# Two small reads move from SyncE's DMA queue to GpSimd's, behind its fill of a zero tile

## The chip, the cores and the metric

The kernel runs on one core of a Trainium2 chip. The metric is the device time in microseconds (us) of one execution; lower is better. Three runs of the kernel before gave 217.78 us as the median, from 217.74 to 218.26.

A core has five engines, which work through their own instruction lists in order and wait for each other through semaphores: TensorE (PE, with PEld for its weight loads), VectorE (DVE), ScalarE (ACT), GpSimd (POOL) and SyncE (SP). SP computes nothing here; it issues transfers. ACT and POOL issue a few transfers too. All transfers run on the core's 16 DMA engines. SBUF is the on-chip memory with 128 partitions, PSUM the memory that TensorE writes to.

## The reference

An attention with polynomial features feeds a token-mixing block. For batch 4, heads 4, sequence 1088 and head size 32:

```python
a = einsum('rd,bhsd->bhsr', S1, x); b = einsum('rd,bhsd->bhsr', S2, x)   # r = 8
phi(x) = outer product of a and b over r, flattened to 64 features
kv  = einsum('bhsf,bhsd->bhfd', phi(k), v);  z = sum over s of phi(k)
att = (phi(q) @ kv) / (phi(q) . z + 1e-6)                    # (4, 4, 1088, 32)
x   = att laid out as (4, 1088, 128)
theta = x @ w_theta
y = w_tok_r @ (x * cos(theta)) + w_tok_i @ (x * sin(theta))  # over the sequence
u = x + y
out = u + max(u @ w_ch, 0)
```

q, k and v are float32. S1, S2 (8 x 32 each) and the weights (two 1088 x 1088, two 128 x 128) come as float64. [...]

## The kernel before, in words

**Order of the work.** The function describes the work as 1,020 operations (`op(engine, duration, function, writes, reads, due, ...)`), numbered in the order of the calls. Two tables written into the file, `ORDER` and `STARTS`, give the order in which the operations are issued and a planned start in hundredths of a us. Each engine runs its operations in that order and waits where data is missing. `STARTS` also decides which buffer of a class an operation gets, and how many filler matmuls TensorE does between operations. The dependencies between them are found from the buffers that they read and write.

**Loads.** q, k and v of a batch come as one transfer of 576 KB each (line 671; the keys of batches 0 and 1 by ACT's queue, line 668; the queries of batch 3 in another layout, line 663). A second copy of the keys of batches 1 to 3 comes at line 714. The token weights come as 17 rows of 1088 KB (line 642, tile zs), the square weights as one transfer of 256 KB (also line 642). SP issues all of them but the two at line 668, in the fixed order. A transfer on SP's or ACT's queue takes one of eight semaphores in turn, so the ninth must wait until the first has landed, the tenth for the second, and so on; POOL's transfers have eight of their own. Those of POOL at line 393 add to what lies in their target.

**The small matrices.** Lines 435 to 472 bring in S1 and S2. `read_heads(E, i0, i1)` issues two reads on the engine E: at line 444 both matrices, transposed by the host to 32 rows of 16 numbers, go to four groups of 32 partitions of tile st (128 rows of 128 bytes, 16 KB); at line 446 S2 as it is goes to 8 partitions (2 KB). DVE clears st first (line 452). Then ACT makes float32 numbers of it (line 459), DVE shifts, masks and joins the words (lines 463 to 468, shown as L383 and L386, the lines of the helpers), ACT converts the low parts (line 471), DVE multiplies (L379). The result is tile sp. From it come the scaled matrices (lines 498 to 540) and sbk, the block matrix with which TensorE makes the features of the keys (`kfeatures`).

```python
src = s_t.rearrange("d t r -> d (t r)").unsqueeze(0).to_broadcast((i1 - i0, D, 2 * R))
E.dma_start(dst[i0 * D:i1 * D, 0:2 * R], src)
if i1 == H:
    E.dma_start(dst[0:R, 2 * R:NS], s_2)
```

**The stages.** Until about 78 us the kernel loads, makes the features, the sums over the keys, the levels of the queries and the attention, and turns the rows of token weights into float32 as they arrive: ACT makes two parts of each row (lines 643 and 645), DVE joins them. TensorE begins the mixing of batch 0 as rows become ready. Then the mixing (`mix_row`, `winograd` for the pair of batches 2 and 3, seven products in place of eight) keeps TensorE occupied up to about 210 us. `mix_out`, `done` and `finish` add x, do the last product and store.

**At the start.** POOL makes an identity matrix (masks.py, tile ident) and fills the tile idle with zeros (line 430, operation 0 of the list). TensorE multiplies these zeros as a warm-up from then on (line 428). ACT issues the keys of batches 0 and 1 and loads an activation table. ACT's first real operation is the sum of squares of batch 0's keys (line 693); the next one in its list is line 459.

Of the kernel before, what the change touches and what calls it, by code (L numbers as in the profile page):

```python
# [138 lines left out]
)  # L139
WARM = 0  # L140
FILL = 5.0
LOAD_LEAD = 60.0
RAW_LEAD = 30.0
CHAINS = ((0,), (1,), (2, 3))
QPOOL = (False,) * 4
# [167 lines left out]
def kernel(  # L313
# [12 lines left out]
    B, _, NC, H, D = q.shape  # L326
# [1217 lines left out]
```

## Time and profile before

| what | value |
|---|---|
| median of 3 runs | 217.78 us (217.74 to 218.26) |
| the profiled execution, its own time | 217.81 us |
| its span, from the first to the last instruction | 215.9 us |
| mean granted TensorE clock | 0.995 |
| PE busy | 208.9 us, 97% of the span |
| DVE busy | 174.3 us, 81% |
| ACT busy | 114.5 us, 53% |
| POOL busy | 59.7 us, 28% |
| SP's DMA queue (q1) | 22868 packets, 31.86 MB |
| ACT's DMA queue (q10) | 3600 packets, 1.62 MB |
| POOL's DMA queue (q0, software) | 1552 packets, 3.25 MB |
| read from HBM | 29.84 MB |

How to read what follows. Line numbers (L459) are those of the kernel. "q" behind an engine's name means its sequencer, which issues transfers and waits. A row of a timeline has the start in us from the first instruction, the duration, the engine, the line, the operation, the tile written and the tiles read, and, in square brackets, how long the engine had been idle before and what ended that. The duration of a transfer's issue is that of the issuing instruction; when the data has landed is told by the semaphore, which the trace holds too. The packets that the DMA engines moved are recorded with queue, start, duration and size. The chain of waits is followed back from the last instruction, at each step to what released it. Averages over the span mix the stage that loads and prepares (to 78 us) with the one in which TensorE multiplies (78 to 210 us).

### The profile page before, as it was taken

The page shows a single profiled execution, that of the slowest core. Times are in us where ns is not written, and L with a number is a line of the kernel's source. Part 1 is how long each engine was busy: PE and PEld are TensorE (multiplying, and loading weights), DVE is VectorE, ACT ScalarE, POOL GpSimd, SP SyncE. Part 2 cuts the span into 40 slices and gives each one's busy share as a digit, 9 for nine tenths or more (in the row PEclk, how much of TensorE's full clock was granted, in tenths as well). Part 3 has the DMA queues.
Part 4 walks back from the last instruction along what each step waited for, and adds up shares of the span by engine and source line. Part 5 has one row for each costly group of instructions (what it writes and reads, how often), then busy time and mean ns, then how long its engine had stood idle before and what let it go on. Part 6 is the DMA issues. An engine that isn't in the chain of part 4 may idle for free.

```text
span 215.9 us, 5832 instructions
## 1 busy us (share of the span) xinstructions
PE 208.9 (97%) x2396; PEld 152.8 (71%) x2396; DVE 174.3 (81%) x343; ACT 114.5 (53%) x256; POOL 59.7 (28%) x105
## 2 busy tenths in 40 slices
PE   7899999999999999999999999999999999999992
PEld 7677798868866666866668666667677776666781
DVE  1799998999999998999999798885994747456263
ACT  4899989999998895798704233363810000000000
POOL 1272740306400000604004100000006489950403
PEclk9999999999999999999999999999999999999998
DMA  6999999995998993192002402424050420010735
GB/s 222 395 418 419 384 365 420 425 315 97 360 285 267 416 432 145 75 308 45 0 0 32 74 3 112 114 109 112 2 88 15 67 39 0 0 23 8 125 55 103
DMA packets 28046, 37.09 MB, mean 172 GB/s; under 512 B 20564, under 2 KB 23044, under 8 KB 25844
## 3 DMA queue, kind: packets, MB, share of 16 engines
q1 hardware_dynamic: 22868, 31.86, 42.4%
q0 software_dynamic: 1552, 3.25, 7.2%
q10 hardware_dynamic: 3600, 1.62, 2.8%
q8 instruction: 19, 0.31, 0.6%
q14 instruction: 7, 0.06, 0.1%
HBM read 29.84 MB, written 4.00 MB: 157 GB/s over the span
## 4 chain that ended last, share of the span: by engine, by line
PE 63%; DMA 18%; ACT 14%; issue 2%; SPq 1%; DVE 1%; POOL 1%; POOLq 0%; ACTq 0%
PE ps L399 61%; DMA zs<-w_tok 13%; DMA big<-k_l 5%; ACT big L645 4%; ACT big L643 3%; ACT lv L1056 1%; PE ps L1131 1%; ACT big L1021 1%; ACT g L1199 1%; ACT g L1202 1%; ACT g L1205 1%; ACT g L1203 1%; POOL out L1299 1%; SPq L671 0%; ACT g L1135 0%
## 5 line engine op out<-in xcount | busy, mean ns | idle before, releaser
L399 PE MATMUL ps<-big,zs 128*128 128x384 f32 (+2 forms) x380 | 110.5, 436 | 0.0
L399 PEld LDWEIGHTS ps<-big,zs 128*128 128x128 f32 x380 | 66.9, 190 | 32.5
L379 POOL TENSOR_TENSOR big<-big,big 128x544 f32<-128x544 f32 x16 | 22.1, 1458 | 48.6 <-DVE big L379 44.6
L399 PE MATMUL ps<-big,big 128*32 128x32 f32 (+2 forms) x352 | 22.8, 234 | 0.0
L643 ACT ACTIVATE big<-zs 128x1088 f32<-128x1088 f32 x17 | 20.9, 1231 | 1.5 <-DMA zs<-w_tok 0.9
L379 DVE CUSTOM_DVE_ANT_0 big<-big,big 128x2176 uint16<-128x2176 uint16 x17 | 21.5, 1275 | 0.0
L645 ACT ACTIVATE big<-zs 128x1088 int32<-128x1088 uint32 (+1 forms) x18 | 21.4, 1194 | 0.3 <-DMA zs<-w_tok 0.3
L1338 ACT COPY big<-ps 80x256 f32<-80x256 f32 x1 | 0.4, 368 | 39.6 <-DMA out<-g 39.6
L399 PEld LDWEIGHTS ps<-big,big 128*32 128x32 f32 (+1 forms) x352 | 15.3, 124 | 6.8 <-issue 0.8
L1276 ACT COPY g<-ps 128x384 f32<-128x384 f32 (+1 forms) x6 | 2.5, 466 | 23.4 <-PE ps L399 23.4
L379 DVE TENSOR_TENSOR big<-big 128x544 f32<-128x544 f32 x8 | 9.5, 1204 | 5.6 <-PE ps L399 5.6
L383 DVE TENSOR_SCALAR big<-big 128x1088 int32<-128x1088 int32 x17 | 12.2, 719 | 0.0
L379 POOL TENSOR_TENSOR mf<-mv,sm 128x32 f32<-128x32 f16 (+1 forms) x3 | 0.8, 262 | 39.1 <-DVE sm L379 39.1
L428 PE MATMUL ps<-idle 128*128 128x112 bf16 (+1 forms) x67 | 10.0, 312 | 1.3 <-POOL idle L430 1.3
L379 DVE TENSOR_TENSOR g<-lv 128x768 f32<-128x768 f32 x12 | 11.1, 950 | 0.1
L399 PEld LDWEIGHTS ps<-w,big 128*128 128x128 f32 (+1 forms) x76 | 9.8, 189 | 1.4
L379 DVE TENSOR_TENSOR big<-big,hf 128x1152 f32<-128x1152 f32 x8 | 10.7, 1351 | 0.0
L399 PE MATMUL ps<-w,big 128*128 128x128 f32 (+1 forms) x76 | 10.5, 278 | 0.0
L399 PE MATMUL ps<-sbk,g 128*128 128x64 f32 x72 | 10.0, 276 | 0.3 <-ACT g L793 0.3
L379 DVE TENSOR_TENSOR zs<-zs,g 128x384 f32<-128x384 f32 (+2 forms) x24 | 9.8, 447 | 0.2
L386 DVE SCALAR_TENSOR_TENSOR big<-ps,even,big 128x384 f32<-128x384 f32 (+1 forms) x10 | 4.8, 493 | 6.3 <-PE ps L399 6.2
L1199 ACT ACTIVATE g<-ps 128x384 f32<-128x384 f32 x12 | 5.9, 504 | 7.3 <-PE ps L399 7.3
(199 smaller groups left out, 379.2 us busy)
## 6 DMA issues: line engine op xcount, KB each, us to landing
zs<-w_tok SPq DMA_DIRECT2D x17, 1088.0 KB, 10.6
big<-k_l SPq DMA_DIRECT2D x5, 576.0 KB, 13.2
big<-v_l SPq DMA_DIRECT2D x4, 576.0 KB, 15.6
big<-q_l SPq DMA_DIRECT2D x3, 576.0 KB, 10.7
big<-hf POOLq DMA_DIRECT2D x3, 576.0 KB, 10.0
far<-zs SPq DMA_DIRECT2D x3, 576.0 KB, 2.8
zs<-far SPq DMA_DIRECT2D x12, 144.0 KB, 4.3
big<-k_l ACTq DMA_DIRECT2D x2, 576.0 KB, 4.4
```

The source lines that it names most:

```text
L379: eng.tensor_tensor(out=o, in0=a, in1=b, op=f)
L383: (eng or V).tensor_scalar(out=o, in0=a, scalar1=s1, scalar2=s2, op0=op0, **kw)
L386: (eng or V).scalar_tensor_tensor(out=o, in0=a, scalar=s, in1=b, op0=op0, op1=op1)
L399: T.matmul(o, lhs, rhs, start=start, stop=stop, skip_group_check=True)
L428: T.matmul(nowhere()[:, :n], idle()[:, 0:P], idle()[:, :n], start=True, stop=True, skip_group_check=True)
L643: op("A", 0.22 + n * 0.0009, lambda: A.activation(dfn(), words_of(raw(), n)[1].bitcast(F32), AF.Prelu, scale=2.0**-112, alpha=-(2.0**32)), ...
L645: op("A", 0.22 + n * 0.0009, lambda: A.activation(stp(), words_of(raw(), n)[0].bitcast(U32), AF.Copy, scale=2.0**-29), [stp], [raw])
L1021: op("A", act(GW) + 0.1, lambda g=g, tr=tr: A.activation(f()[:, g * GW:(g + 1) * GW], tr(), AF.Copy, scale=s()[:, 0:1]), [(f, g)], [tr, (s ...
L1056: op("A", act(480), lambda g=g, lp=lp: A.copy(lv().rearrange("p l (c n) -> p l c n", n=HR)[:, :, g * GC:(g + 1) * GC], lp().rearrange("p c ...
L1131: T.transpose(tr()[:, i * P:(i + 1) * P], qp()[:, i * H + 2 * n:i * H + 2 * n + 2].rearrange("p h i j -> p (h i j)"), ident())
L1199: op("A", act(GW), lambda cs=cs, th=th: A.activation(cs()[:, 0], th(), AF.Copy, bias=ROUND), [(cs, 0)], [th])
L1276: op("A", act(w), lambda: A.copy(u(), yp()[:, :w]), [uT], [yp])
```

## The change

The two reads at lines 444 and 446 are issued by POOL instead of SP. Operation 0, POOL's fill of the zero tile, is moved ahead in the list, so that it still comes first on POOL; its planned start changes to 0.90 us, the other operations keep theirs. SP's list is the same but for the two reads: its first transfer is now the keys of batch 3.

```diff
 ORDER = (
-    29, 32, 4, 2, 5, 0, 1, 3, 34, 30, 356, 50, 33, ...
+    29, 32, 4, 0, 2, 5, 1, 3, 34, 30, 356, 50, 33, ...
 STARTS = (
-    73, 73, 90, 92, 103, 130, 170, 220, 358, ...
+    73, 73, 90, 90, 92, 103, 170, 220, 358, ...
...
-        op("S", 0.1, lambda: read_heads(SY, 0, H), [(st, 0)], [], due=-4000.0, lk=H + 1)
+        op("S", 0.1, lambda: read_heads(G, 0, H), [(st, 0)], [], due=-4000.0, lk=H + 1)
```

Of the operations named: 29 and 32 are ACT's key loads, 4 clears st, 0 fills the zero tile, 2 sets constants on DVE, 5 is the pair of reads, 1 is the warm-up, 3 the first activation, 34 SP's load of batch 3's keys, 30 that of batch 0's queries.

118 rows, old and new, of tables (ORDER, STARTS) are left out of this document.

## The prediction

> **What bounds the kernel now.** I read the chain of waits first, then the busy time by stage, then the two timelines of ScalarE (ACT) and VectorE (DVE) over the first 40 us, and last the DMA packets of the first 8 us. In the chain of waits (start, us, what) these pieces are the frame:
>
> ```profile
> 3.63 11.58 DMA big<-k_l
> 15.22 16.38 DMA zs<-w_tok
> 31.63 0.62 ACT big L643
> ...
> 123.58 86.46 PE ps L399 x601
> ```
>
> The end is set by TensorE, which runs almost without a hole from 78 us on. What precedes it is set elsewhere. The busy times by stage (stretch, its length, then busy PE, PEld, DVE, ACT, POOL) say where:
>
> ```profile
> 6.60:15.00 8.40, 7.44 (x166) 5.73 (x165) 7.73 (x26) 7.92 (x24) 4.23 (x16) 1.00 1.03 417
> 15.00:31.60 16.60, 16.31 (x303) 13.22 (x301) 16.18 (x37) 15.26 (x40) 7.86 (x22) 1.00 1.03 393
> 35.00:78.00 43.00, 42.63 (x773) 32.22 (x775) 42.24 (x79) 40.74 (x82) 8.00 (x17) 1.00 0.94 324
> ```
>
> DVE is busy 42.24 of the 43.00 us before the TensorE stage (the PE column holds idle-time matmuls too), and DMA runs at a share of 1.03 up to 31.6 us. So before 78 us a delay of DVE or ACT has nothing to hide under, except where they wait for something else. The timelines of both show every such place of 0.5 us or more between 4 and 40 us (start, duration, group, then idle before it and its releaser):
>
> ```profile
> 4.56 1.17 ACT L693 ACTIVATE big<-big 128x1152 f32<-128x1152 f32 x1 [1.44 <-DMA big<-k_l]
> 6.37 0.24 ACT L459 ACTIVATE sp<-st 128x48 f32<-128x48 f32 x1 [0.55 <-DMA st<-s]
> ...
> 31.63 1.23 ACT L643 ACTIVATE big<-zs 128x1088 f32<-128x1088 f32 x1 [0.58 <-DMA zs<-w_tok]
> ```
>
> ```profile
> 6.65 0.19 DVE L383 TENSOR_SCALAR sp<-sp 128x48 int32<-128x48 int32 x1 [4.49 <-ACT sp L459]
> ...
> 35.10 0.46 DVE L383 TENSOR_SCALAR big<-lv 128x576 f32<-128x576 f32 x1 [0.56 <-ACT lv L1056]
> ```
>
> So the small read, which lands in tile st, gates both: ACT L459 starts 0.09 us after its landing at 6.28, and DVE 0.28 us after that start. From 6.65 to 34.55 DVE has no hole. At 31.05 ACT runs out of work and waits 0.58 for a weight row, and DVE then waits 0.56 for ACT. **The rule I use:** if the first stage starts D later, the first 0.55 us of D vanish in those two waits, whose end is set by DMA; the rest reaches the end one for one.
>
> **The change, part by part.** *SP loses two issues.* The issues before (SP's own queue; start, duration):
>
> ```profile
> 0.98 0.74 SPq L444 DMA_DIRECT2D st<-s_t  x1
> 1.78 0.44 SPq L446 DMA_DIRECT2D st<-s  x1
> 2.27 0.38 SPq L671 DMA_DIRECT2D big<-k_l  x1
> ```
>
> SP waited for DVE's clearing of st (ends 0.95); its entry semaphore came at 0.64, as ACT's did, and ACT issued at 0.72. So SP's first big load (keys of batch 3, 576 KB) moves from 2.27 to about 0.72, 1.55 us. That buys no transfer time by itself: the packets show ACT's two key loads filling all 16 engines from 1.76 to about 5.3 us, and no SP packet before 5.23, though the small reads had been issued by 2.22. Later issues wait for landings eight DMAs back (w_sq at 4.55, a q load at 6.12); with two DMAs fewer these waits lift earlier, but always behind a backlog. Hence 0 for the rest of SP's queue. One gain is possible: over 5.25 to 6.25 us the packets carry some 0.11 MB less than at the 390 GB/s after it, 0.28 us, in the stretch with the 136 small packets. It counts only if the first stage isn't late.
>
> *The price on ACT's first load.* Batch 0's keys (issued by ACT at 0.72, landed 4.54) now meet SP's 576 KB issued in the same 0.01 us. ACT's second load, which today stands in line behind the first, lands from 5.59 to 6.21: that is what batch 0's keys get if SP's load goes first or the two share the engines. Bounds: 0 to +1.67 us. I take 5.9, the middle of 5.59 to 6.21, because two of the three orders give it: L693 then starts 5.92, ACT is free 1.26 later (as 4.56 to 5.82 today), at 7.18, so D = 7.18 - 6.37 = 0.8. The second key load would land at about 8.2 instead of 6.2 and is used at 8.42: covered by ACT's own work, which is late too.
>
> *POOL gets two issues.* It is free at once after its start-up:
>
> ```profile
> 0.86 0.42 POOL L430 MEMSET idle<- 128x384 bf16 x1
> 1.34 0.28 POOL masks.py:199 TENSOR_SCALAR_AFFINE_SELECT ident<-ident 128x128 f32<-128x128 f32 x1
> 8.00 0.79 POOL L379 TENSOR_TENSOR s<-sp 128x16 f32<-128x16 f32 x1 [6.37 <-DVE sp L379]
> ```
>
> Issues start at 1.3 to 1.6 us; one of 128-byte rows (L1299) takes 0.60 to 0.70, so the second starts at 1.9 to 2.3. TensorE's warm-up waits for the fill alone, which stays ahead; the identity (first used 4.86) has 2 us to spare even behind the issues; POOL's next work waits for the read anyway. What the trace lacks is a small POOL read under a full DMA. The nearest rows (KB each, us to landing) bound it:
>
> ```profile
> big<-hf POOLq DMA_DIRECT2D x3, 576.0 KB, 10.0
> ...
> out<-g POOLq DMA_DIRECT2D x7, 48.0 KB, 2.5
> ```
>
> From idle engines 2.0 is the shortest L1299 landing: 1.9 + 2.0 = 3.9 at best. Beside full engines a 576 KB accumulating transfer took 10.0: 2.3 + 10.0 = 12.3 at worst. In packets, those three loaded transfers sent their first one 4.1 to 4.6 us after the issue, against 1.4 to 1.8 idle, and then took turns with SP's. The 128-byte rows of POOL's stores go out as packets of 3072 bytes (24 rows at once), SP's one by one at 128 bytes, so I count the read as one packet per engine, not 32 turns. First packet 1.9 + 4.1 to 2.3 + 4.6 = 6.0 to 6.9, plus 0.5 to the semaphore (5.76 to 6.28 today): 6.5 to 7.4. I take 7.0: D = 7.0 + 0.09 - 6.37 = 0.7.
>
> A rule speaks for the order before: the Trainium skill, DMA: Bandwidth & Descriptors, Issuing engine by pattern, gives simple loads to Sync and calls its path generally faster, with about 1 us to the first byte from GpSimd against 0.6. By that the read would be 0.4 later, plus 0.3 for the later issue: 7.0, an estimate from that page and the start times; the trace's own rows (1.4 to 1.8 idle against 1.05 for ACT's first load) agree in sign.
>
> *Sum.* The two delays overlap: ACT needs both, so the later counts. I take D = 0.95, a little over the larger (0.8) since either may be the later one. Past the slack: 0.95 - 0.55 = **+0.4 us**. The profiled execution took 217.81 (span 215.9 and 1.9 around it), 0.03 over the median 217.78: **218.2 us**.
>
> **The rivals.** *Nothing is lost* (217.8): ACT's load goes first and the read lands by 6.8, so D is under 0.55 and the wait for the weight row swallows it. For it: the queues of ACT and SP so far served whole loads in order. Against it: SP's load is no longer issued later.
>
> *The read is late by a whole turn* (slower, 219.2): it must queue behind what the engines hold and then give way again between its own packets and semaphores. Price: first packet at 2.3 + 4.6 = 6.9, then some of the 1.1 to 2.1 us between the first and the last semaphore of those loaded transfers, say 1.3, so 8.2: D = 1.9, +1.4. If its 32 rows each waited for a 4608-byte packet (0.178 us), 32 x 0.19 = 6 us more than the 6.0 of a first packet: 12, near the worst row, +5.2, 223. It decides from a landing at about 7.5 on. For it: 10.0 against 2.5 above. Against it: the 3072-byte packets.
>
> *The stream starts fuller* (faster, 216.9): between 1.75 and 3.0 us the engines moved 229 KB where 475 KB would fit, 0.63 us. Two loads at once might fill that; with the 0.28 above, the weight row would land 0.9 sooner, at 30.7, and ACT and DVE, 0.55 earlier through an early read, would use it. It decides when L643 starts before 31.0. Against it: the first packets took 0.4 to 0.9 us each instead of 0.178, a slow start that more requests need not cure. The Trainium skill, same page, Queues, rings and completion order, has each engine go round-robin between queues by packets. By that the small read passes the backlog and lands near 4.5, which helps this rival, though batch 0's keys then share with SP's load. Today's SP packets, 3 us behind ACT's, don't show such turns; POOL's do.
>
> **How the numbers follow.** Forecast 0.44, nothing lost 0.16, read late 0.32, fuller start 0.08. What this kernel's measurement tells from no change is about 0.3%, 0.65 us. The forecast case spans +0.1 to +0.9 (D of 0.65 to 1.45) and passes 0.65 in a fifth of its chance: slower 0.32 + 0.09 = 0.41; within 0.44 x 0.8 + 0.16 = 0.51; faster 0.08. The range 217.3 to 219.6 leaves out some 0.06 below and 0.13 above (the 12 us landing and its neighbours).
>
> **What would show it.** L693's start (4.56 now; 5.9 forecast; unchanged if ACT's load goes first); L459's start (6.37; 7.1 to 7.5) and whether st or L693 released it; DVE's first L383 moved alike; the waits at 31.63 and 35.10 gone with those starts moved by 0.4; packets of the software queue at 6 to 7 us, few and large. I'm wrong if L459 moves and the waits at 31.63 and 35.10 stay, since then DMA was not what ended them, or if L459 is on time and the time still moves.

## The result and the profile after

The changed kernel takes 220.6 us (median of 6 executions, 219.91 to 223.01), the kernel before 217.98 beside it on the same chip (6, 217.74 to 218.26). The ratio is 1.0126, 95% interval 1.0097 to 1.0156: slower by 2.75 us, where 0.4 was forecast. The profiled execution is the shortest of the six: 219.91, span 218.0. The ratios are those of undisturbed executions alone, which in some experiments puts the median of all above the ratio.

SP's first load and POOL's first issue stand where the forecast had them, POOL's second 0.17 us behind its bounds of 1.9 to 2.3 (timelines of SP and POOL after; start, duration):

```profile
0.72 0.40 SPq L671 DMA_DIRECT2D big<-k_l  x1
```

```profile
1.58 0.88 POOL L444 DMA_DIRECT2D st<-s_t  x1
2.47 0.55 POOL L446 DMA_DIRECT2D st<-s  x1
```

What came of them is in the timelines of ACT and DVE after, at the instructions shown of before:

```profile
6.47 1.16 ACT L693 ACTIVATE big<-big 128x1152 f32<-128x1152 f32 x1 [3.31 <-DMA big<-k_l]
...
8.78 0.25 ACT L459 ACTIVATE sp<-st 128x48 f32<-128x48 f32 x1 [1.05 <-DMA st<-s]
...
33.48 1.24 ACT L643 ACTIVATE big<-zs 128x1088 f32<-128x1088 f32 x1
```

```profile
9.06 0.19 DVE L383 TENSOR_SCALAR sp<-sp 128x48 int32<-128x48 int32 x1 [6.90 <-ACT sp L459]
...
37.15 0.46 DVE L383 TENSOR_SCALAR big<-lv 128x576 f32<-128x576 f32 x1
```

Batch 0's keys release L693 at 6.47 instead of 4.56. When ACT is through with them, it waits another 1.05 us for the small read, and L459 starts at 8.78 instead of 6.37: **D is 2.41 us**. L643 and DVE's second mark have no bracket any more: both waits are gone, as the rule demands. L643 is 1.85 later than before (2.41 less its wait of 0.58 would be 1.83), DVE's mark 2.05 (1.86 by the rule), and the profiled execution ends 2.10 later. The chain of waits after says the same in fewer words:

```profile
2.47 6.23 DMA st<-s
...
29.45 7.07 PE ps L399 x119
...
125.57 86.46 PE ps L399 x601
```

The two long pieces of key and weight loads that stood in the chain of before are not in it; a DMA of 2 KB is, with 6.23 us. The last piece, TensorE's 86.46 us of mixing, is as long as before and starts 1.99 later. By stage, the loss is all at the front (after; stretch, length, then busy PE, PEld, DVE, ACT, POOL):

```profile
6.60:15.00 8.40, 8.15 (x150) 6.43 (x152) 5.52 (x20) 6.87 (x18) 2.10 (x5) 1.00 1.03 411
15.00:31.60 16.60, 16.17 (x296) 12.61 (x282) 16.06 (x36) 16.02 (x41) 8.36 (x26) 1.00 1.02 400
35.00:78.00 43.00, 43.00 (x743) 32.88 (x740) 42.33 (x79) 41.24 (x86) 7.73 (x17) 1.00 0.93 320
```

DVE does 5.52 us of work in the first stretch where it did 7.73; in the two others it is as busy as before.

The landings, by the semaphores of the trace: batch 0's keys 6.45 (4.54 before), SP's keys of batch 3, issued in the same 0.01 us, 6.25; the first small read 7.97 (6.11), the second 8.69 (6.28). The packets of POOL's queue begin at 6.03. The stream behind is earlier, not later: the keys SP issues fourth land at 13.53 instead of 15.21, and the weight row that L643 waited for at 29.08 instead of 31.61. Nobody can use it, since ACT and DVE are late.

### The profile page after: what moved, and what is told of

It reads as the page before. It is cut to its first block, busy times and chain, and to the rows that moved or that the text cites. A ratio compares the mean times of both kernels' runs of the same rounds, so it can differ in the third digit from the quotient of the medians.

```text
span 218.0 us, 5834 instructions
## 1 busy us (share of the span) xinstructions
PE 210.5 (97%) x2396; PEld 153.8 (71%) x2396; DVE 174.6 (80%) x343; ACT 114.2 (52%) x256; POOL 60.9 (28%) x107
## 4 chain that ended last, share of the span: by engine, by line
PE 86%; ACT 6%; DMA 3%; POOL 1%; DVE 1%; issue 1%; POOLq 0%; ACTq 0%
PE ps L399 81%; DMA st<-s 3%; PE ps L1131 2%; ACT big L693 2%; PE ps L1018 1%; ACT g L793 1%; ACT big L1021 1%; PE ps L428 1%; ACT big L991 1%; ACT big L645 1%; ACT big L643 1%; POOL out L1299 0%; PE ps L1189 0%; POOL st L444 0%; PE ps L790 0%
## 5 line engine op out<-in xcount | busy, mean ns | idle before, releaser
L643 ACT ACTIVATE big<-zs 128x1088 f32<-128x1088 f32 x17 | 20.9, 1231 | 0.5 <-DVE lv L379 0.5
L428 PE MATMUL ps<-idle 128*128 128x112 bf16 (+1 forms) x67 | 10.7, 324 | 1.3 <-POOL idle L430 1.3
```

Source lines behind the costliest of these rows:

```text
L428: T.matmul(nowhere()[:, :n], idle()[:, 0:P], idle()[:, :n], start=True, stop=True, skip_group_check=True)
L643: op("A", 0.22 + n * 0.0009, lambda: A.activation(dfn(), words_of(raw(), n)[1].bitcast(F32), AF.Prelu, scale=2.0**-112, alpha=-(2.0**32)), ...
```

## The experiments

The theory after the result: the loss is D less 0.55, and D comes from two things, keys that share the engines with SP's load, and a read on POOL's queue that lands late under load. Rivals: one of the two alone; the freed SP queue (a stream that collides elsewhere); TensorE's clock.

**1. SP's load ahead of SP's own reads** (the kernel before, operation 5 behind 34). It brings the collision of the key loads without POOL's queue.

```diff
-    29, 32, 4, 2, 5, 0, 1, 3, 34, 30, ...
+    29, 32, 4, 2, 0, 1, 3, 34, 5, 30, ...
```

> The kernel before with one edit: SP issues its first key load ahead of the two small reads, not behind them. The reads stay on SP. This sets the price of the collision of ACT's and SP's first loads by itself. Theory (two delays, the later counts): batch 0's keys share the engines packet by packet with SP's load and land near 6.4 instead of 4.5; the reads stand behind SP's load and land near 7; ACT is free at 7.7, so L459 starts at 7.7 instead of 6.4, and 0.8 to 1.0 us of that reaches the end: 218.8 to 219.0. Rival A (only POOL's read costs, the late keys are covered): no change, 218.0. Rival B (SP's early load is the whole loss): as the changed kernel, 220 or more.

Measured: 219.33 us, ratio 1.0048 (1.0030 to 1.0067). The keys land at 6.32, but the reads at 7.96 and 8.15, later than expected, on SP's queue too. L459 of this kernel:

```profile
8.24 0.25 ACT L459 ACTIVATE sp<-st 128x48 f32<-128x48 f32 x1 [0.64 <-DMA st<-s]
```

So the price of the keys was not measured by itself here. What follows is that POOL's queue isn't needed for a late read: here two reads on SP's queue, issued behind a big load on the same queue, landed 1.85 and 1.87 later than before.

**2. POOL's reads, with SP as late as before.** SP issues the same two reads to a tile that nobody uses, so its big loads start where they did.

```diff
-        st = fixed((NS,), I64, "st")
+        st, st2 = fixed((NS,), I64, "st"), fixed((NS,), I64, "st2")
...
-... lambda: read_heads(G, 0, H), [(st, 0)] ...
+... lambda: (read_heads(G, 0, H), read_heads(SY, 0, H, st2)), [(st, 0)] ...
```

> The changed kernel, but SP still issues the same two reads at its old place, into a tile that nobody uses, so that its first big load goes out as late as before. This sets the price of POOL's read by itself. Theory: batch 0's keys land near 4.5 as before; POOL's first packet goes out about 4.4 us after its issue, near 6.0, and the last semaphore comes 1.5 to 2.7 us later, 7.5 to 8.7; L459 starts at 7.6 to 8.8, 1.2 to 2.4 late, of which 0.8 to 2.0 reach the end: 218.8 to 220.0. Rival B (SP's early load is the whole loss): the read lands near 6.3 and the time is 218.0.

Measured: ratio 1.0035 (1.0009 to 1.0060), by four of six executions; all six lie from 218.64 to 224.2, median 219.41. The keys land at 4.70, near the 4.54 of before. In one and the same execution SP's reads land at 6.35 and 6.52, POOL's at 7.73 and 8.09:

```profile
8.18 0.24 ACT L459 ACTIVATE sp<-st 128x48 f32<-128x48 f32 x1 [2.20 <-DMA st<-s]
```

The late read, with the keys only 0.16 late, makes D = 1.81.

**3. One read instead of two** (the second is left out; the columns for S2 stay zero).

```diff
-        if i1 == H:
+        if i1 > H:
             E.dma_start(dst[0:R, 2 * R:NS], s_2)
```

> The changed kernel without its second read (S2 in its natural layout is left out, those columns of the tile stay zero). It asks what the 2.7 us between POOL's first packet and the last semaphore consist of. Theory (turns: each packet and each semaphore of POOL's queue waits for a turn on every engine): one read has half of them; it lands near 8.0, where the first read's last semaphore came, instead of 8.7, L459 starts at 8.1, and the time is 0.7 us under the changed kernel's, near 219.9. Rival (a fixed delay of a transfer issued by POOL under load): the one read lands as late as the pair did, L459 near 8.8, no change from the changed kernel.

Measured: ratio 1.0051 (1.0029 to 1.0073), by four of six executions; all six lie from 219.27 to 222.77, median 219.57. The one read lands at 8.21, no earlier than the first of two (7.97). The second read costs about 0.5 to 0.7 us behind the first (8.69 in the kernel after), not more. L459 then waits for the first read alone:

```profile
8.23 0.24 ACT L459 ACTIVATE sp<-st 128x48 f32<-128x48 f32 x1 [0.68 <-DMA st<-s_t]
```

**4. POOL's reads ahead of its fill and of the identity** (only the columns from 2R on are cleared, so that the first read needn't wait for the clearing).

```diff
-    29, 32, 4, 0, 2, 5, 1, 3, 34, 30, ...
+    29, 32, 4, 5, 0, 2, 1, 3, 34, 30, ...
...
-... lambda: G.memset(idle(), 0.0), [idle] ...
+... lambda: (G.memset(idle(), 0.0), make_identity(nc, ident.ap)), [idle] ...
...
-... lambda: V.memset(st().bitcast(F32), 0.0), [st] ...
+... lambda: V.memset(st()[:, 2 * R:].bitcast(F32), 0.0), [st] ...
```

> The changed kernel with POOL's reads ahead of its fill and its identity, and the clearing of the tile cut to the columns that the first read doesn't write, so that the first read waits for nothing and is issued near 0.72 us, together with ACT's and SP's first loads, not at 1.58. Theory (a queue that comes to busy engines waits some 4.4 us for its first packet, one that comes to idle engines 1.4): the read now comes while the engines start; it lands between 3.5 and 5, before batch 0's keys, which still share with SP's load and land near 6.3; L459 at 7.6, 1.2 late: 218.9 to 219.2. Rival (4.4 us is what a POOL transfer costs here whatever it meets): first packet near 5.1, landing near 7.8, L459 at 7.9: 219.2 to 219.5. The landing tells them apart, not the time.

Measured: 220.12 us, ratio 1.0105 (1.0090 to 1.0120). POOL issues at 1.27, not at the 0.72 that was expected, so a read that starts together with the first loads wasn't had here; both forecasts of the landing were too early. Against the 1.58 of the kernel after, the first packet goes at 5.94 (6.03), and the reads land later, at 8.36 and 9.09. So the place behind the fill, which the title names, shows no cost: 0.31 us of earlier issue bought no earlier landing. L459 of this kernel:

```profile
9.18 0.24 ACT L459 ACTIVATE sp<-st 128x48 f32<-128x48 f32 x1 [1.51 <-DMA st<-s]
```

**5. Batch 0's and 1's keys on SP's queue** (the kernel after, line 668 issued by SP, ahead of its other loads). Nothing shares with batch 0's keys now.

```diff
-            op("A", 0.44, lambda: A.dma_start(t()...
+            op("A", 0.44, lambda: SY.dma_start(t()...
```

> The changed kernel with ACT's two key loads issued by SP too, ahead of SP's others: one hardware queue instead of two. Theory (queues take turns by packets, one queue serves its loads in order): batch 0's keys land near 4.4, the second keys near 5.9; POOL's read has one rival queue instead of two, so its turns come twice as often: last semaphore near 7.5 instead of 8.7; L459 at 7.5 to 7.7, 1.1 to 1.3 late; 0.6 to 1.0 reach the end: 218.6 to 219.0. Rival (the engines serve loads in the order of issue whatever the queue): the keys gain nothing by the common queue, and the time stays at the changed kernel's 220 or more.

Measured: ratio 1.0079 (1.0027 to 1.0130), by three of six executions, 218.96, 219.12 and 222.0; the other three took 222.64 to 224.49, at mean clocks of 0.968 to 0.977. In the execution of 219.12 the keys land at 4.47, as before the change, POOL's reads still at 7.81 and 8.03, not at the 7.5 expected from one rival queue instead of two:

```profile
4.49 1.17 ACT L693 ACTIVATE big<-big 128x1152 f32<-128x1152 f32 x1 [2.27 <-DMA big<-k_l]
...
8.12 0.24 ACT L459 ACTIVATE sp<-st 128x48 f32<-128x48 f32 x1 [2.37 <-DMA st<-s]
```

The collision of the keys is taken away and D is still 1.75. Both parts together made 2.41, so the shared keys go with about 0.6 to 0.7 more on a delay that the read makes by itself. A second profile of this kernel is used below:

> The kernel with all key loads on SP once more, for one look, in the hope of a profile of one of its long executions. If it is long: by the theory of the clock, POOL's read lands near 8 as in the short execution and TensorE's half-clock stretch reaches 8 to 12 us further; by the rival the read lands 3 us later or more and the half-clock stretch follows from it.

It took 221.02, though the reads landed at 7.88 and 8.08 and L459 started at 8.17 as in the short one (8.12): its extra 1.9 us are not a later landing.

**6 and 7. More filler matmuls**, to keep TensorE's clock up during the longer wait: 12 more at the start and 24 ahead of the transpose at line 482, in the kernel after and in that of experiment 5.

```diff
-[spin(112) for _ in range(39)]
+[spin(112) for _ in range(51)]
...
-... lambda: T.transpose(t()[:n, :P], mfn(), ident()), [t], [m])
+... lambda: ([spin(112) for _ in range(24)], T.transpose(t()[:n, :P], mfn(), ident())), [t], [m])
```

> The changed kernel with more of TensorE's filler matmuls: 51 for 39 at the start and 24 before the first transpose that waits for the small matrices (L482), where TensorE was idle. In the changed kernel's profile TensorE ran at half clock until 10.8 us, before at full clock from 5.6 on, and single executions of all kernels with POOL's reads took 222 to 224 us at a mean granted clock of 0.968 to 0.983. Theory (TensorE's idle time while the first stage waits lets the clock stay or fall to half, in some executions for long): with the fillers all executions stay near the best ones of the changed kernel, 219.3 to 220.3, at a clock of 0.995 or more. Rival (the long executions come from POOL's transfer landing late, the clock only follows): the fillers change nothing, some executions take 222 us or more.

> The kernel with all key loads on SP (four of its six executions took 222 us or more, at a clock of 0.968 to 0.982), with the same added filler matmuls. Theory (idle TensorE, then half clock): none over 220, median near 219.0. Rival (late landings in those executions): half of them over 222 again.

Measured: 223.23 us, ratio 1.0252 (1.0219 to 1.0284), and 224.72, ratio 1.0322 (1.0291 to 1.0352). Both are slower than without the fillers, so the test says nothing about the clock. The waits of experiment 6, then of 7 (engine, line, releaser: sum, times, longest) show why:

```profile
PE ps L399 <- issue: 3.8, 2, 2.6
```

```profile
PE ps L399 <- issue: 3.5, 2, 2.3
```

In 6, in its longest execution (225.96), TensorE stands for 1.22 us at 41.2 and for 2.62 at 62.3 with nothing shown that it waits for; in 7 for 1.22 at 40.2 and 2.26 at 59.9, in an execution at full clock from 6.5 us on that is 3.8 longer than the profiled one of 5. The kernel after has no such hole. In both traces the holes come behind the same number of TensorE's instructions, 1473 and 2241 as recorded, which speaks for a place in its list and against a moment. What delays the instructions there stays open.

**8. Wider fillers, not more of them.**

```diff
-[spin(112) for _ in range(39)]
+[spin(154) for _ in range(39)]
```

> The kernel after, with its 39 first filler matmuls 154 instead of 112 columns wide: no instruction is added, and TensorE's fillers should end at about 6.5 instead of 5.16 us, where it waited 1.42 us for the keys. Theory (the longer executions, 220.4 to 223.0, come from half-clock time after TensorE's idle wait): L459 stays at 8.7 to 9.1, the clock is full from 5 to 7 us on (10.8 in the profiled execution after), every execution lies within 219.2 to 220.1, median 219.6. Rival (they come from a later landing or from the stream of loads): the executions still spread from 219.9 to 223, median about 220.6, mean clocks down to 0.983. Second rival (fillers cost time themselves, as the added ones did by holes of 1 to 2.6 us that show no releaser): 221 or more, with such holes between 40 and 65 us.

Measured: 221.31 us (220.26 to 223.05), ratio 1.0134 (1.0110 to 1.0158). The forecast of my theory fell: the first wait was filled, but TensorE then waited 2.15 us at 8.45 for the small matrices:

```profile
10.61 0.27 PE L482 MATMUL ps<-ident,m 128*2 128x128 f32 x1 [2.15 <-DVE m L501]
```

The profiled execution, 223.03, shows half the clock from 12.4 us on, in the column of the granted clock behind POOL's:

```profile
12.40:19.20 6.80, 6.80 (x119) 5.96 (x117) 4.29 (x11) 4.25 (x13) 3.31 (x17) 0.50 1.03 413
```

The same stretch of the kernel after:

```profile
12.40:19.20 6.80, 6.80 (x152) 5.30 (x151) 6.42 (x17) 6.67 (x18) 4.86 (x17) 1.00 1.02 412
```

At half the clock TensorE gets 119 matmuls done instead of 152, and DVE, which waits for ACT's copies of their results, 4.29 us of work instead of 6.42: 2.13 us lost, of the 3.1 by which this execution exceeds the profiled one after; another 0.42 is L459's later start. The second profile of experiment 5 has the same picture with one such window: TensorE busy 1.23 of 3.40 us, then half the clock for 3.50.

```profile
6.30:9.70 3.40, 1.23 (x11) 0.76 (x10) 1.15 (x9) 1.08 (x4) 0.00 (x0) 1.00 1.04 412
9.70:13.20 3.50, 3.50 (x43) 2.68 (x42) 3.25 (x10) 3.03 (x8) 1.07 (x2) 0.51 1.00 403
```

**9. SP's first read at once** (the kernel before, clearing only from column 2R on, so that the read is issued at 0.72 instead of 0.98).

```diff
-... lambda: V.memset(st().bitcast(F32), 0.0), [st] ...
+... lambda: V.memset(st()[:, 2 * R:].bitcast(F32), 0.0), [st] ...
```

> The kernel before, clearing only the columns of st that the first read does not write, so that SP can issue that read at about 0.72 us, with ACT's first key load, instead of 0.98. Theory (a queue that starts with another shares the engines with it packet by packet; one that starts 0.26 us later, as the read of before did, waits until the other's loads are through): the first read lands at 3 to 5 us instead of 6.1, batch 0's keys at 4.6 to 4.9, L459 starts right behind L693 at 5.8 to 6.2, and the end is 0 to 0.5 us earlier, 217.4 to 217.9 beside 217.9. Rival (ACT's queue goes first whatever the start): landing 6.0 to 6.3 as before, L459 at 6.3 to 6.4, time within 0.2 of before.

Measured: 217.82 us, ratio 0.9980 (0.9967 to 0.9993), by nine of ten executions (the tenth took 220.89). The first read lands at 4.87 instead of 6.11: issued together with ACT's load, its packets go from 3.90 on between ACT's; issued 0.26 us later, none went before 5.23. The second, issued at 1.52, still lands at 6.25 and holds L459 at 6.33, not at the 5.8 to 6.2 expected. What gain there is comes with the earlier stream: the weight row lands at 30.86 instead of 31.61, and L643, at 30.88, no longer waits for it. The profiled execution takes 217.82 all the same (217.81 before). L459 of this kernel:

```profile
6.33 0.24 ACT L459 ACTIVATE sp<-st 128x48 f32<-128x48 f32 x1 [0.52 <-DMA st<-s]
```

**10. The reads on ACT's queue, the keys on SP's** (experiment 5, the reads issued by ACT at 0.73 with the clearing of experiment 9, operations 4 and 5 first in the list). No software queue, and SP's stream starts at 0.72.

```diff
-op("S", 0.1, lambda: read_heads(G, 0, H), ...
+op("A", 0.1, lambda: read_heads(A, 0, H), ...
```

> The kernel after, but the small reads are issued by ACT's queue at about 0.72 us (only the columns that the first read does not write are cleared), and the keys of batches 0 and 1 by SP's, ahead of its other loads. It is meant as a version that could beat both: no software queue, and SP's stream starts at 0.72. Theory (queues that start together share packet by packet): the first read lands at 3 to 5.5 us, batch 0's keys at 4.5 to 5.2, L459 right behind L693 at 5.9 to 6.5; with the stream of loads some 0.5 us earlier the waits at 31 and 35 us shrink and the time is 217.3 to 218.0. Rival (the queue with the long loads goes first): the reads land at 7.8 or later, L459 at 8 or later, 219 to 219.5, as with keys on SP and the reads on POOL.

Measured: 218.22 us beside 218.07, ratio 1.0005 (0.9985 to 1.0024). The reads land at 5.04 and 6.82:

```profile
4.63 1.17 ACT L693 ACTIVATE big<-big 128x1152 f32<-128x1152 f32 x1 [0.82 <-DMA big<-k_l]
...
6.91 0.24 ACT L459 ACTIVATE sp<-st 128x48 f32<-128x48 f32 x1 [1.02 <-DMA st<-s]
```

The first read is as early as expected, the second is not, so L459 starts at 6.91 (5.9 to 6.5 expected) and nothing is gained. Here D is 0.54 and nothing is lost, as the rule says of a D under 0.55. It also speaks against the freed SP queue as a cause: the loads behind land when they do in the kernel after (the first weight row at 12.12 against 12.11, the second key load of line 671 at 13.56 against 13.53).

**11. POOL's reads on idle engines** (every load is held back until both have landed: L459 and a small copy out of st come before them). The total, 222.41, means nothing.

```diff
-    29, 32, 4, 0, 2, 5, 1, 3, 34, 30, ...
+    4, 0, 2, 5, 1, 3, 6, 29, 32, 34, 30, ...
...
-... lambda: A.activation(sp()[:, 0], words()[1]...
+... lambda: (SY.dma_start(st2()[0:R], st()[0:R]), A.activation(sp()[:, 0], words()[1]...
```

> The kernel after, with every load held back until the two small reads have landed: L459 and ACT's key loads behind it, and SP's loads behind a small copy out of st. Its total time means nothing (all loads start late); it measures POOL's reads on idle engines. Theory (the 4.45 us from the first issue to the first packet and the 2.66 us from there to the last semaphore are the price of the loads already in flight): first packet 1.4 to 1.8 us after the issue, as POOL's stores at 168 to 204 us had it, at about 3.2, and the last semaphore at 3.9 to 4.8. Rival (the software queue is this slow at the start of a program, or with this pattern of 128 rows, whatever else moves): first packet at 5.5 to 6.1, landing at 7 or later.

Issued at the same 1.58 and 2.46, the reads send their first packet at 3.10 and have landed at 3.84 and 4.13. The rows of DMA issues (KB each, us to landing), first of the kernel after, then of this one:

```profile
st<-s_t POOLq DMA_DIRECT2D x1, 16.0 KB, 6.4
st<-s POOLq DMA_DIRECT2D x1, 2.0 KB, 6.2
```

```profile
st<-s_t POOLq DMA_DIRECT2D x1, 16.0 KB, 2.3
st<-s POOLq DMA_DIRECT2D x1, 2.0 KB, 1.7
```

The same two transfers take 2.3 and 1.7 us alone, 6.4 and 6.2 under the loads: 4.1 to 4.5 us are the load's price. Of the second read's, 2.92 lie before the queue's first packet (6.03 against 3.10) and 1.6 between that packet and the last semaphore (2.66 against 1.03). The Trainium skill, DMA: Bandwidth & Descriptors, Anatomy of one DMA — SWDGE (gpsimd) path, fits about 2.0 us and a term by bytes to such a transfer. The trace agrees on idle engines, and is three times that under load.

## Why the prediction was wrong, step by step

**The rule for D held in the main.** The first number column is L459's start; D is that less 6.37; the rule takes 0.55 off; the last column is (ratio - 1) times the median of before on the same chip.

| kernel | L459 | D | by the rule | measured, us (interval) |
|---|---|---|---|---|
| after | 8.78 | 2.41 | 1.86 | 2.75 (2.1 to 3.4) |
| 1, SP's load first | 8.24 | 1.87 | 1.32 | 1.05 (0.65 to 1.5) |
| 2, SP as late as before | 8.18 | 1.81 | 1.26 | 0.76 (0.2 to 1.3) |
| 3, one read | 8.23 | 1.86 | 1.31 | 1.11 (0.6 to 1.6) |
| 4, reads before the fill | 9.18 | 2.81 | 2.26 | 2.29 (2.0 to 2.6) |
| 5, keys on SP | 8.12 | 1.75 | 1.20 | 1.72 (0.6 to 2.8) |
| 8, wide fillers | 9.20 | 2.83 | 2.28 | 2.92 (2.4 to 3.4) |
| 9, SP at once | 6.33 | -0.04 | 0 | -0.44 (-0.7 to -0.15) |
| 10, reads on ACT | 6.91 | 0.54 | 0 | 0.11 (-0.3 to 0.5) |

Six of the nine values by the rule lie in the interval. Two that don't, after and 8, are under its lower end by 0.25 and 0.1 (the kernel lost more than the rule says), and 9 gained what the rule does not give. Experiments 6 and 7 are not in the table: they lost 5.5 and 7.0 us, with holes of 3.8 and 3.5 in the profiled executions that D doesn't explain. The forecast fell short by 2.35 us (2.75 against 0.4). Of this 1.46 is the wrong D (1.86 against 0.4); 0.24 more was lost in the profiled execution (2.10 against 1.86), and the rest, 0.65, lies between that execution and the others.

**The failed step is the read's landing: "plus 0.5 to the semaphore".** Its first half was nearly right: issues at 1.58 and 2.47, the 16 KB in four packets of 4096 bytes beside smaller ones, the first packet at 6.03 (6.0 to 6.9 forecast). From there to the last semaphore the prediction took 0.5 us; it is 2.66, and the landing 8.69 instead of 7.0. The 0.5 comes from SP's reads of before, but 5.76 is their last packet, not their first (5.23); up to the last semaphore, 6.28, the same stretch was 1.05 there, and it is 1.03 for POOL's reads alone (experiment 11). So the time from the first data packet to the last was put at nothing, by counting one packet per engine. It is 1.81 after (6.03 to 7.84) and 0.67 alone; the rest, to the last semaphore, is 0.86 and 0.35.

That each of these pieces waited for its turn again under load is how I read it: the 64 packets of the two reads, semaphores included, start over 2.2 us instead of 0.7, while SP's and ACT's queues move 0.43 and 0.42 MB from 6.0 to 8.25. The prediction had this as its rival "the read is late by a whole turn" (landing 8.2, 219.2). The 1.1 to 2.1 us that it took from POOL's other transfers run from the first semaphore to the last; for the pair of reads this is 1.6, and another 1.06 lies between the first packet and the first semaphore. So the rival had the mechanism, and its 8.2 is near by luck in part: a first packet too late (6.9) and a step too short (1.3). The forecast should have used those rows, which are of the same queue, instead of a row of SP's. With 2.66 in place of 0.5, and the first packet at 6.03, the sum is D = 8.78 - 6.37 = 2.41, +1.86.

**The price on ACT's keys** was put at 5.9, in bounds of 0 to +1.67; it is 6.45, +1.91. The two loads shared packet by packet and ended almost together (6.25 and 6.45). The bound was the landing of the second of two such loads before, 6.21; why the pair ends up to 0.24 later when it shares isn't shown. This alone gives 6.47 + 1.26 = 7.73, D = 1.36 instead of 0.8, and it hides behind the read.

**"The two delays overlap"** is right only in part: alone, the late read makes 1.75 to 1.81 (5 and 2), with the shared keys 2.41. That the same sharing leaves more load in flight ahead of the read would explain it; no run separates this.

**"Hence 0 for the rest of SP's queue"** holds: experiment 10 starts SP's stream at 0.72 too, its loads land as in the kernel after up to 14 us, and it is level with before. The rival "the stream starts fuller" had half of its mechanism right, the weight row landed 2.5 earlier, but its condition, a first stage on time, failed. "Nothing is lost" was wrong for this kernel and describes experiment 10.

**TensorE's clock had no term.** The six executions after spread from 219.91 to 223.01, mean clock from 1.0 to 0.983. In experiment 8 and in the second profile of 5, half-clock windows follow TensorE's idle wait, and DVE loses 2.13 us in the first of the two. That the longer executions after have the same cause is argued from these two; they were not traced themselves. It would account for the 0.7 between the shortest execution and the median. In the profiled execution itself the clock was at half until 10.8 us (5.6 before; the nine matmuls of line 790 take 2.15 us instead of 1.46), but TensorE's first matmuls on DVE's features come 2.41 later, just D, so up to there it cost nothing (before, then after):

```profile
8.76 0.35 PE L399 MATMUL ps<-hf 128*32 128x32 bf16 x28 [0.23 <-DVE hf L383]
```

```profile
11.17 0.35 PE L399 MATMUL ps<-hf 128*32 128x32 bf16 x28
```

## What to carry to other kernels

A small read that gates the first stage belongs in front of the big loads, started with them or ahead: in one trace of each, 0.26 us later cost it 1.2 us of landing on SP's queue (4.87 against 6.11), and POOL's queue under full engines made 2 us into 6. When a queue is freed, look at what now starts earlier on it and which load on the path it will share the engines with. Take the price of a transfer from rows of the same queue, up to its last semaphore: here the first packet came 4.45 us after the first issue, and the last semaphore 2.66 after that.

## What the runs showed of the hardware

- Two queues of ACT and SP that start together share by packets (576 KB each: landed at 6.45 and 6.25, against 4.54 with no other queue; from 3.25 to 5.75 us each moved the same 0.51 MB). The Trainium skill, DMA: Bandwidth & Descriptors, Queues, rings and completion order, says that each engine goes round its queues by packets; for loads that start together the trace agrees. A queue that starts 0.26 us later didn't get such turns before (first read 6.11, when ACT's two loads were nearly through); why is open.
- Under load the first packet of POOL's reads went at 5.91 to 6.05 in the kernel after and in experiments 3 to 8, whether the issue began at 1.27 or 1.58, at 5.14 where SP's small reads preceded its loads (experiment 2), and at 3.10 alone. What it waits for until then stays open.
- TensorE's clock falls in windows. Experiment 8: full from 5.6, half from 12.4, full from 19.3; the second profile of 5: full from 6.3, half from 9.7, full from 13.2: steps of 3.4 or 6.8. Waits of 2.15 and 2.17 us were followed by half the clock in these two, and one of 2.83 (experiment 5, first profile) was not. The Trainium skill, TensorE: Matmul & The Clock Gate, Part 1, gives a window of about 3.4 us that runs free of the kernel; the steps agree, and a free phase would explain why the same wait is dear in one execution and free in another. Counted in steps of 3.41 us from the recorded changes, TensorE is busy for 1.6 us (8) and 1.2 (second profile of 5) of the step ahead of the fall, and the 2.83 us lie across two steps with 2.0 and 1.8. That is no threshold: in experiment 6 a step with 1.6 was followed by full clock and one with 2.2 by half.
- In experiments 6 and 7 the 36 added fillers went with two holes far behind them, 1.22 us at 40 to 41 and 2.3 to 2.6 at 60 to 62, behind the same instructions of TensorE and with no releaser shown.
